# The opening of a chunked recurrence with three layers behind it, issued in another order

## The chip, the core and the metric

The kernel runs on one core of a Trainium2 chip. Its time is device time in microseconds (us), from the first instruction of the program to the last, and the number quoted for a kernel is the median of several executions. The engines are named as in the profile: PE is TensorE (matmuls, with PEld its weight loads), DVE is VectorE, ACT is ScalarE, POOL is GpSimd and SP is SyncE, which here only issues transfers. Each engine takes its instructions strictly in the order in which the program holds them.

## What is computed

A recurrence over 768 steps for 4 batches of 8 heads, with states of 40x40, whose output is the input of a gated two-matrix layer, whose output in turn goes through a layer of eight experts with top-1 routing. Cut to what matters:

```python
for t in range(S):                                   # 768 steps, per batch and head
    y[:, :, t] = einsum('bhd,bhde->bhe', rt, state)
    Sa = einsum('bhde,bhe->bhd', state, at)
    state = state * wt[:, :, None, :] - einsum('bhd,bhe->bhde', Sa, bt)
    state = state + einsum('bhd,bhe->bhde', vt, kt)
x = ((x @ w_a) * (x @ w_b)) @ w_out                  # 3072 tokens, 320 -> 1536 -> 320
out[mask] = gate_w * (relu(x[mask] @ w1[e]) @ w2[e]) # the expert of each token, 8 experts
```

## The kernel before

The recurrence is cut into 12 chunks of 64 steps. Within a chunk it becomes matmuls, and what one step does to the next inside the chunk is undone by inverting a triangular 64x64 matrix for each of the 32 pairs of batch and head. Work on chunk c runs in 24 slots; inside the same slots the program also prepares chunk c+2, inverts for a later chunk, and, from chunk 1 on, runs the first layer's matmuls (groups `pm`) for the chunk before. The order of PE, DVE, ACT and POOL is the order in which the Python code emits instructions. SP's transfers are put in order by a scheduler.

The steps that the text speaks of, for one chunk:

- `load_w`, `load_bk`: the decay `w` and the pair `b`,`k` are loaded (366 KB and 720 KB). `scans`: DVE runs a scan over `w` backwards, copies sums, takes reciprocals and scans again; before that POOL writes ones into the tile `d`, of which there is one.
- `scale_a`: the `a` of a chunk (two halves of 180 KB, each for a pair of batches) is scaled by POOL and spread by three transfers into the block tile `ablk`. There is one `ablk` for each pair, so the spread of the next chunk waits for the score matmuls of this one. `scale_bk`: DVE scales `b` and `k`.
- `scores`: 3 matmuls for each of 4 batches (`s1p`); ACT copies each result into `s`; POOL masks half of it; SP sends a quarter to DRAM as `nd` (four transfers of 64 KB for a chunk).
- `tinv`: `nd` is read back as `m`, twice 256 KB, each row to two partitions, and then DVE does the inverse as 31 pairs of a multiply and a subtract (`tmp`, `xt`), each on what the one before left. The last one sends `xt` to DRAM as `td` and reads it back into `s`.
- `t21a`, `t21b`: from the two inverted corners the third is made, with PE (`ta`, `tb`), ACT and DVE. Only then can the stages (`stage0` to `stage5`: `px`, `pu`, `pv`, `pp`, `p`, `py`, `pz`) of the chunk run.
- `rows` turns `bk` around (`kbp`, `kb`), `relayout` moves the decay into the layout of the output (`gp`, six transfers), `spans` lets ACT check the range of the decay (`junk`).

Beside this the two weight matrices of the first layer must be split into two 32-bit parts. `weight_steps` does that in 30 pieces; a piece is one load (`raw`, issued by ACT), four DVE instructions (`c_f`, `c_s`, `c_f`, `c_s`), three or more of ACT and two or three of POOL, and is emitted in four steps, which `conv.take(n)` deals out. The groups `pm` of chunk 0 run in chunk 1's slots and need the pieces in order.

Ahead of the slots, in `phase1`, stands the opening. In the kernel before it loads, scans and scales both chunks 0 and 1 first, then emits 20 steps of conversion, then chunk 0's scores, 5 steps, chunk 0's `rows`, 10 steps, chunk 1's scores, and then both inverses, which are dealt out on DVE in turns, together with 40 more steps. Thus 75 of the 120 steps stand ahead of chunk 0's slots, and 44 within them.

Of the kernel before, what the change touches and what calls it, by code (L numbers as in the profile page):

```python
# [8 lines left out]
F32 = mybir.dt.float32  # L9
# [123 lines left out]
def phase1(tc, I, cst, drm, psA, psM, ident, hT, mk_ident, wo, xs, span, tiny, down):  # L133
# [17 lines left out]
    sp = A.p2.tile([128, 2 * 256], I32, tag="raw", name="sp0"), A.p2.tile([128, 2 * 256], I32, tag="raw", name="sp1")  # L151
    A.load(0)
    A.load(1, M.room())
# [5 lines left out]
    A.setup()  # L159
    run(A.spans(1))  # L160
    A.scale_a(0, 0)
    A.scale_a(0, 1)
    run(A.scale_bk(0))
    run(A.scans(1))
    for pr in range(2):
        A.scale_a(1, pr, spread=False)
    run(A.scale_bk(1))
    n0, n1, n2, n3 = FIRST["conv0"]
    A.zero([A.vnt])
# [3 lines left out]
    run(conv.take(n0))  # L173
    for b in range(B):
        A.scores(0, b)
        if b % 2:
            A.spread_a(1, b // 2)
    run(conv.take(n1))
    for b in range(B):
        A.rows(0, b)  # L180
    tinv = A.tinv(0)
    run(conv.take(n2))
# [5 lines left out]
    mix(tinv[:n3], conv.take(FIRST["conv1"][0]) + [lambda b=b: A.rows(1, b) for b in range(B)])  # L188
    t1 = A.tinv(1, (uh, view(xt)))
    A.relayout(0)  # L190
    A.relayout(1)
    lead = FIRST["lead"]
    both = tinv[n3:n3 + lead]
    tinv = tinv[n3 + lead:]
    while tinv or t1:
        both += tinv[:1] + t1[:1]
        tinv, t1 = tinv[1:], t1[1:]
    mix(both, [lambda b=b: A.stage0(0, b) for b in range(2)] + conv.take(FIRST["conv1"][1]))
    run(A.spans(0, [t[:120, 0:L // 2].bitcast(F32) for t in sp]))
    units, tinv = [], []  # L200
    for c in range(NCH + 1):
# [9 lines left out]
        for i in range(24):  # L211
# [96 lines left out]
    if not down:  # L308
# [32 lines left out]
        0, 3, 3, 2, 3, 2, 2, 2, 2, 1, 2, 2,  # L341
        2, 2, 2, 4, 1, 1, 3, 0, 3, 0, 1, 1],
    "conv0": [20, 5, 10, 16], "conv1": [10, 30], "lead": 5, "early": 12, "load": 0, "bk": 5, "sa": [3, 5], "score": [9, 12, 13, 15], "row": [12, 13, 23, 23],
    "t21a": [8, 9, 14, 15], "t21b": [9, 12, 18, 16], "tinv": [0] * 24, "relayout": 17, "load_w": 18,
# [43 lines left out]
class Attention:  # L388
# [48 lines left out]
    def load(self, c, room=None):  # L437

        w, bk = room if room else (None, None)
        self.load_w(c, w)  # L440
        self.load_bk(c, bk)
# [58 lines left out]
    def scale_a(self, c, pr, spread=True):  # L500
        nc = self.nc
        st = self.st[c]
        t = self.p2.tile([120, 6 * 64], F32, tag=f"at{pr}", name=f"at{c}_{pr}", bufs=2 + pr)[:, :6 * C]
        sr = self.src("a", "a", c)[:, 6 * C * pr:6 * C * pr + 6 * C]
        nc.sync.dma_start(t, sr)
# [4 lines left out]
        if spread:  # L510
            self.spread_a(c, pr)

    def spread_a(self, c, pr):
        for m in range(3):
            self.nc.sync.dma_start(
                self.ablk[pr][m * D:(m + 1) * D, :, :, m, 0:C], self.st[c]["at"][pr][m * D:(m + 1) * D])
# [1208 lines left out]
```

## Time and profile before

| what | value |
|---|---|
| times shown, 3 runs | 1346.05, 1346.48, 1353.48 us; median 1346.48 |
| the profiled execution | 1349.91 us, of which the span of its instructions is 1348.2 |
| PE busy | 1192.2 us, 88% of the span |
| DVE busy | 679.9 us, 50% |
| ACT busy | 531.7 us, 39% |
| POOL busy | 444.0 us, 33% |
| granted TensorE clock, mean | 0.911 of full speed |

Over the whole span PE is the busy engine. The opening is another picture: in the first 100 us PE has next to nothing to do, and the other engines and the transfers decide when it can start. A row of a timeline gives start, duration, engine, line, operation, the tiles written and read, how many instructions are merged into the row, and in square brackets how long the engine had been idle and what ended that.

### The profile page before, as it was taken

Reading aid. Unit: us, or ns where it says so; the run is one execution under the profiler, and the core shown is the slowest. Engines: PE = TensorE matmul, PEld = TensorE weight load, DVE = VectorE, ACT = ScalarE, POOL = GpSimd, SP = SyncE. Lnnn points to the kernel's source line nnn. Section 1 sums busy time; section 2 is a strip of 40 time slices with the busy share of each in tenths; the row PEclk is TensorE's granted clock in tenths of the full one; section 3 lists DMA queues with packets and bytes.
Section 4 is the critical chain, followed back from the end, with each engine's and each line's share of the span. In section 5 each row is a group of like instructions: output and inputs, shape, how many; then the busy total and the mean of one; then the engine's idle time right before and its main releaser. Section 6 shows DMA issues by size and latency. Waiting matters only on the chain.

```text
span 1348.2 us, 27424 instructions
## 1 busy us (share of the span) xinstructions
PE 1192.2 (88%) x10474; PEld 1120.2 (83%) x10474; DVE 679.9 (50%) x1867; ACT 531.7 (39%) x1301; POOL 444.0 (33%) x488
## 2 busy tenths in 40 slices
PE   2306879997999998998999999999999989999995
PEld 2305779896888898898989999999999989999995
DVE  7487456563746465564746545312355685222321
ACT  3435544343343434352534333332333434444541
POOL 5443531232232323232421211112012255666650
PEclk9655559999998898998989999999799999999998
DMA  7363343537564748564544432217255635545420
GB/s 188 87 163 80 82 108 94 124 98 153 119 151 117 157 121 151 128 159 104 122 117 99 115 86 76 66 49 207 75 161 174 214 131 183 164 131 174 130 69 16
DMA packets 252908, 166.63 MB, mean 124 GB/s; under 512 B 158674, under 2 KB 236195, under 8 KB 252769
## 3 DMA queue, kind: packets, MB, share of 16 engines
q1 hardware_dynamic: 238545, 141.17, 41.1%
q0 software_dynamic: 9808, 15.76, 4.2%
q10 hardware_dynamic: 4416, 7.87, 2.1%
q8 instruction: 85, 1.39, 0.4%
q14 instruction: 54, 0.44, 0.1%
HBM read 111.76 MB, written 44.60 MB: 116 GB/s over the span
## 4 chain that ended last, share of the span: by engine, by line
PE 66%; DMA 15%; DVE 7%; issue 4%; POOL 3%; ACT 3%; SPq 1%; POOLq 0%; DVEq 0%; ACTq 0%
PE pm L964 19%; PE py L1101 8%; PE dn L1410 5%; PE u L1390 5%; DMA hT<-uh 4%; PE py L797 3%; PE px L716 3%; PE s1p L535 3%; PE p L775 3%; DMA at<-in_a 3%; PE pp L757 2%; PE py L793 2%; PE pu L735 2%; PE px L713 2%; PE ta L652 2%
## 5 line engine op out<-in xcount | busy, mean ns | idle before, releaser
L976 DVE TENSOR_TENSOR uh<-pm,ua 128x256 f32<-128x256 f32 x144 | 60.7, 422 | 249.3 <-PE pm L964 235.0
L964 PE MATMUL pm<-xl,wh 128*128 128x256 f32 x576 | 144.5, 333 | 0.5 <-POOL xl L943 0.5
L612 DVE TENSOR_TENSOR tmp<-m,xt 128x126 f32<-128x126 f32 (+22 forms) x372 | 116.4, 316 | 29.2 <-DMA m<-nd 14.6
L782 POOL TENSOR_SCALAR_AFFINE_SELECT s<-s 64x512 f32<-64x512 f32 x96 | 73.0, 760 | 140.7 <-ACT s L780 135.6
L964 PE MATMUL pm<-xh,wl 128*128 128x256 f32 x576 | 118.8, 289 | 0.0
L964 PE MATMUL pm<-xh,wh 128*128 128x256 f32 x576 | 118.0, 287 | 0.0
L618 DVE TENSOR_TENSOR xt<-xt,tmp 128x126 f32<-128x126 f32 (+22 forms) x372 | 111.0, 302 | 7.6
L1393 DVE SCALAR_TENSOR_TENSOR hl<-u,hh 128x384 fp32r<-128x384 f32 (+5 forms) x72 | 41.6, 581 | 140.7 <-ACT hh L1392 140.7
L943 POOL TENSOR_TENSOR xl<-xf,xh 128x192 fp32r<-128x192 f32 x48 | 28.7, 599 | 245.3 <-ACT xh L942 221.5
L967 ACT COPY ua<-pm 128x256 f32<-128x256 f32 x144 | 53.6, 372 | 124.1 <-PE pm L964 119.1
L652 PE MATMUL ta<-t,s 32*32 32x32 f32 x768 | 34.6, 202 | 69.0 <-DVE t L649 60.0
L964 PEld LDWEIGHTS pm<-xl,wh 128*128 128x128 f32 x576 | 90.3, 197 | 6.3 <-POOL xl L943 0.7
L1101 PE MATMUL py<-wh,hl 128*128 128x328 f32 x288 | 91.4, 317 | 2.1 <-DVE hl L1091 2.1
L1101 PE MATMUL py<-wl,hh 128*128 128x328 f32 x288 | 92.5, 321 | 0.6 <-DVE wl L1072 0.6
L964 PEld LDWEIGHTS pm<-xh,wh 128*128 128x128 f32 x576 | 92.4, 197 | 0.0
L964 PEld LDWEIGHTS pm<-xh,wl 128*128 128x128 f32 x576 | 92.3, 196 | 0.0
L1101 PE MATMUL py<-wh,hh 128*128 128x328 f32 x288 | 91.1, 316 | 0.0
L652 PEld LDWEIGHTS ta<-t,s 32*32 32x32 f32 x768 | 30.7, 117 | 71.5 <-ACT junk L472 41.4
L964 PE MATMUL pm<-xh,w 128*128 128x256 f32 x288 | 83.1, 289 | 0.0
L964 PE MATMUL pm<-xl,w 128*128 128x256 f32 x288 | 83.0, 288 | 0.0
L535 PE MATMUL s1p<-ablk,bk 120*128 120x192 f32 (+1 forms) x264 | 54.2, 350 | 26.0 <-DMA ablk<-at 21.6
L1410 PE MATMUL dn<-l,hh 128*128 128x320 f32 (+3 forms) x240 | 74.9, 312 | 0.0
(240 smaller groups left out, 3108.5 us busy)
## 6 DMA issues: line engine op xcount, KB each, us to landing
hT<-uh SPq DMA_DIRECT2D x72, 256.0 KB
hf<-hT SPq DMA_DIRECT2D x36, 512.0 KB
r<-in_moe_w SPq DMA_DIRECT2D x8, 1280.0 KB
r<-in_moe_w SPq DMA_DIRECT2D x8, 1024.0 KB
bk<-in_bk SPq DMA_DIRECT2D x11, 720.0 KB
xs<-zt SPq DMA_DIRECT2D x8, 805.0 KB
m<-nd SPq DMA_DIRECT2D x22, 256.0 KB
at<-in_a SPq DMA_DIRECT2D x24, 180.0 KB
```

The costliest lines, as they stand in the source:

```text
L535: nc.tensor.matmul(ps[:2 * C, 3 * g * C:(3 * g + n) * C], st["bk5"](b, g), self.ablk[b // 2][:, b % 2, g, 0:n, 0:C], start=True, stop=True)
L612: nc.vector.tensor_tensor(box[0], m[2 * s // R][:, s % (R // 2):s % (R // 2) + 1, s + 1:].to_broadcast([128, rows, n]), xt[:, :rows, s:s + ...
L618: nc.vector.tensor_tensor(xt[:, :rows, s + 1:], xt[:, :rows, s + 1:], box[0], op=ALU.subtract)
L652: nc.tensor.matmul(pa[R:C, R * h:R * h + R], s1[0:R, h, R:C], t11[:, h, :], start=True, stop=True)
L782: nc.gpsimd.affine_select(out=s2t[q * C:q * C + C], in_=s2t[q * C:q * C + C], pattern=[[0, 8], [1, C]], base=0, channel_multiplier=-1, com ...
L964: nc.tensor.matmul(p, l, r, start=(i == 0), stop=(i == len(seq) - 1))
L967: nc.scalar.copy(a, p)
L976: nc.vector.tensor_tensor(h[:, f % 2], p, a, op=ALU.mult)
L1101: self.nc.tensor.matmul(py, self.pair[i][l][:, k, s], self.W[r][:, first + k, cols], start=(first + k == 0 and n == 0), stop=(first + k == ...
L1390: nc.tensor.matmul(p, l, r, start=(i == 0), stop=(i == len(seq) - 1))
L1393: nc.vector.scalar_tensor_tensor(out=hl, in0=p, scalar=0.0, in1=hh.bitcast(F32), op0=ALU.max, op1=ALU.subtract)
L1410: nc.tensor.matmul(p, l[:, q], r[:, f], start=(f == 0 and i == 0), stop=(f == len(hs) - 1 and i == 2))
```

## The change

The opening is emitted in another order. First come chunk 0's `w`, its `a`, its `bk`, and then chunk 1's; `a` is now loaded by a function of its own. Chunk 0 is scanned, scaled, and its `a` is spread, one half by SP and the other by ACT's queue. Then chunk 0's scores and the request for its inverse follow at once, and only then chunk 1's scan and scaling, chunk 0's `rows`, 15 steps of conversion, chunk 1's scores, the first stage of two batches, the whole inverse of chunk 0 in one piece, and chunk 1's `rows`. Chunk 1's inverse is no longer part of the opening: it is dealt out over the slots 0 to 10 of chunk 0, and the `t21` steps of chunk 1 move to the slots 14 to 19. 72 steps of conversion now stand in chunk 0's slots, and the other 33 fall into the first eight of chunk 1. The check of chunk 0's decay moves from the end of the opening to slot 23 of chunk 0.

```diff
-    A.load(0)
-    A.load(1, M.room())
+    A.load_w(0)
+    for pr in range(2):
+        A.load_a(0, pr)
+    A.load_bk(0)
+    room = M.room()
+    A.load_w(1, room[0])
+    for pr in range(2):
+        A.load_a(1, pr)
+    A.load_bk(1, room[1])
...
     A.setup()
+    A.zero([A.vnt])
+    A.scale_a(0, 0)
+    A.scale_a(0, 1, queue=nc.scalar)
+    run(A.scale_bk(0))
     run(A.spans(1))
-    A.scale_a(0, 0)
-    A.scale_a(0, 1)
-    run(A.scale_bk(0))
+    for b in range(B):
+        A.scores(0, b)
+    tinv = A.tinv(0)
     run(A.scans(1))
     for pr in range(2):
-        A.scale_a(1, pr, spread=False)
+        A.scale_a(1, pr)
     run(A.scale_bk(1))
-    n0, n1, n2, n3 = FIRST["conv0"]
-    A.zero([A.vnt])
     A.begin(0)
     for pr in range(2):
         A.vload(0, pr)
-    run(conv.take(n0))
-    for b in range(B):
-        A.scores(0, b)
-        if b % 2:
-            A.spread_a(1, b // 2)
-    run(conv.take(n1))
     for b in range(B):
         A.rows(0, b)
-    tinv = A.tinv(0)
-    run(conv.take(n2))
+    run(conv.take(FIRST["conv0"]))
...
     for b in range(B):
         A.scores(1, b)
-    mix(tinv[:n3], conv.take(FIRST["conv1"][0]) + [lambda b=b: A.rows(1, b) for b in range(B)])
     t1 = A.tinv(1, (uh, view(xt)))
-    A.relayout(0)
-    A.relayout(1)
-    lead = FIRST["lead"]
-    both = tinv[n3:n3 + lead]
-    tinv = tinv[n3 + lead:]
-    while tinv or t1:
-        both += tinv[:1] + t1[:1]
-        tinv, t1 = tinv[1:], t1[1:]
-    mix(both, [lambda b=b: A.stage0(0, b) for b in range(2)] + conv.take(FIRST["conv1"][1]))
-    run(A.spans(0, [t[:120, 0:L // 2].bitcast(F32) for t in sp]))
-    units, tinv = [], []
+    for b in range(2):
+        A.stage0(0, b)
+    run(tinv)
+    for b in range(B):
+        A.rows(1, b)
+    for c in range(2):
+        A.relayout(c)
+    tinv = t1
+    units = []
...
+            if c == 0 and i == FIRST["span0"]:
+                sp = [A.p2.tile([128, 2 * 256], F32, tag="raw", name=f"sp{h}")[:120, 0:L // 2] for h in range(2)]
+                run(A.spans(0, sp))
...
-    "t21a": [8, 9, 14, 15], "t21b": [9, 12, 18, 16], "tinv": [0] * 24, "relayout": 17, "load_w": 18,
+    "t21a": [14, 14, 17, 17], "t21b": [16, 16, 19, 19], "tinv": [5, 6, 6, 6, 6, 6, 6, 6, 6, 6, 3] + [0] * 13, "relayout": 17, "load_w": 18,
...
+    def load_a(self, c, pr):
+        t = self.p2.tile([120, 6 * 64], F32, tag=f"at{pr}", name=f"at{c}_{pr}", bufs=2 + pr)[:, :6 * C]
+        self.nc.sync.dma_start(t, self.src("a", "a", c)[:, 6 * C * pr:6 * C * pr + 6 * C])
+        self.st[c]["raw_a", pr] = t
+
+    def scale_a(self, c, pr, queue=None):
...
-            self.nc.sync.dma_start(
+            (queue or nc.sync).dma_start(
                 self.ablk[pr][m * D:(m + 1) * D, :, :, m, 0:C], self.st[c]["at"][pr][m * D:(m + 1) * D])
```

Three places of the printed order show what moves. The first is ACT in the opening, where chunk 0's score copies stand (`s_0_0`, `s_0_1` are its two pairs of batches; `raw`, `c_s`, `wh` and `w` belong to the conversion). Before:

```order
L870 DMA raw_0_1_247<-in_moe_w_a 128x512
L363 ACTIVATE c_s<-raw_0_2_218 128x256
L370 ACTIVATE c_s,tiny<-c_s,tiny 128x256
L372 CAST w_0_249<-c_f 64x256
L372 CAST w_0_250<-c_f 64x256 x2
L382 CAST w_0_249<-c_f 64x256
L382 CAST w_0_250<-c_f 64x256
L543 COPY s_0_0_271<-s1p_0_267 128x512
L543 COPY s_0_0_271<-s1p_1_274 128x512
```

Now:

```order
L514 DMA ablk_95<-at_1_114 40x6x64 x3
L470 ACTIVATE junk,span<-w_r,wlim 120x384 x4
L542 COPY s_0_0_172<-s1p_0_168 128x512
L542 COPY s_0_0_172<-s1p_1_175 128x512
L542 COPY s_0_1_187<-s1p_2_183 128x512
L542 COPY s_0_1_187<-s1p_3_190 128x512
L568 COPY kb_0_229<-kbp_0_225 128x360
```

Five pieces of conversion stood ahead of the copies; now no piece does, and the spread of chunk 0's second half does instead.

The second place is SP's queue around chunk 0's `m`. Before (`at_0_173` and `at_1_176` are chunk 1's `a`, `s_0` is chunk 0):

```order
L515 DMA ablk_94<-at_0_173 40x6x64 x3
L550 DMA nd_116<-s_0_0_271 32x16x32 x2
L550 DMA nd_116<-s_0_1_289 32x16x32 x2
L515 DMA ablk_95<-at_1_176 40x6x64 x3
L603 DMA m_346<-nd_116 64x1x1024 x2
L550 DMA nd_123<-s_1_0_389 32x16x32 x2
```

Now (`at_0_123`, `at_1_125` are chunk 1's `a`):

```order
L581 DMA gp_492<-w_110 64x4x64 x2
L549 DMA nd_118<-s_0_0_172 32x16x32 x2
L549 DMA nd_118<-s_0_1_187 32x16x32 x2
L514 DMA ablk_94<-at_0_123 40x6x64
L602 DMA m_198<-nd_118 64x1x1024 x2
L514 DMA ablk_94<-at_0_123 40x6x64 x2
L514 DMA ablk_95<-at_1_125 40x6x64 x3
L581 DMA gp_499<-w_r 120x4x64
```

Chunk 0's `m` now has one spread transfer of chunk 1 ahead of it, and five behind it; chunk 0's six `gp` transfers have moved ahead of `nd`.

The third place is SP's queue around the sending of chunk 0's inverse (`td_0`). Before:

```order
L505 DMA at_1_1083<-in_a 120x384
L699 DMA r_0_1529<-in_r 120x192
L699 DMA r_1_1562<-in_r 120x192
L505 DMA at_1_1684<-in_a 120x384
L629 DMA td_0_103<-xt_347 512x1x32 x2
```

Now (`nd_129` and `m_0`, `m_1` are chunk 1's):

```order
L549 DMA nd_129<-s_1_1_329 32x16x32 x2
L581 DMA gp_499<-w_r 64x4x64
L597 DMA m_0_307<-nd_129 64x1x512
L597 DMA m_1_308<-nd_129 64x1x512
L597 DMA m_0_307<-nd_129 64x1x512
L597 DMA m_1_308<-nd_129 64x1x512
L628 DMA td_0_103<-xt_199 512x1x32 x2
```

Chunk 1's four `m` transfers stood far ahead of `td_0`, with the loads of chunks 2 and 3 between; now they stand directly ahead of it.

## Rows read from the trace of the kernel before

**Rows 1.** Timeline of the opening: SP's issues (start, duration, engine, line, tiles).

```profile
15.41 11.64 SPq L515 DMA_DIRECT2D ablk<-at  x6
38.75 1.95 SPq L550 DMA_DIRECT2D nd<-s  x4
43.94 1.29 SPq L603 DMA_DIRECT2D m<-nd  x2
62.46 2.40 SPq L598 DMA_DIRECT2D m<-nd  x4
64.91 10.52 SPq L582 DMA_DIRECT2D gp<-w  x5
104.41 2.63 SPq L629 DMA_DIRECT2D td<-xt  x4
```

**Rows 2.** Timeline of the opening: what the other engines do, and what they waited for.

```profile
8.78 1.78 DVE L496 TENSOR_TENSOR_SCAN w<-w,d 120x780 f32<-120x780 f32 x1
13.29 1.81 POOL L507 TENSOR_TENSOR at<-at,w 120x384 f32<-120x384 f32 x2 [4.85 <-DMA at<-in_a]
15.20 1.79 DVE L492 TENSOR_TENSOR_SCAN suf<-w_r,d 120x781 f32<-120x781 f32 x1 [2.21 <-POOL d L483]
19.36 2.36 POOL L507 TENSOR_TENSOR at<-at,w_r 120x384 f32<-120x384 f32 x2 [4.19 <-DVE w_r L496]
21.64 3.75 PE L535 MATMUL s1p<-ablk,bk 120*128 120x192 f32 x12 [21.64 <-DMA ablk<-at]
37.65 2.06 ACT L543 COPY s<-s1p 128x512 f32<-128x512 f32 x4
38.36 2.50 POOL L544 TENSOR_SCALAR_AFFINE_SELECT s<-s 64x512 f32<-64x512 f32 x4 [1.60 <-ACT s L543]
61.48 0.19 DVE L612 TENSOR_TENSOR tmp<-m,xt 128x31 f32<-128x31 f32 x1 [12.74 <-DMA m<-nd]
112.83 1.88 PE L652 MATMUL ta<-t,s 32*32 32x32 f32 x32 [41.32 <-DVE t L649]
```

**Rows 3.** The chain that ended last: two transfers on it (start, duration).

```profile
51.89 10.55 DMA nd<-s
63.66 12.10 DMA m<-nd
```

**Rows 4.** Busy time by stretch (from:to, length, PE, PEld, DVE, ACT, POOL, clock, DMA share, GB/s).

```profile
56.00:58.00 2.00, 0.00 (x0) 0.00 (x0) 0.00 (x0) 0.00 (x0) 0.00 (x0) 0.52 0.13 49
61.40:104.40 43.00, 1.89 (x16) 1.78 (x16) 36.70 (x136) 16.35 (x46) 19.90 (x19) 0.50 0.55 140
112.60:152.00 39.40, 35.49 (x370) 33.37 (x371) 24.98 (x46) 22.90 (x68) 15.60 (x20) 0.59 0.30 71
152.00:187.80 35.80, 26.39 (x182) 23.18 (x180) 13.29 (x31) 17.53 (x53) 14.09 (x21) 0.50 0.48 113
187.80:209.00 21.20, 21.20 (x138) 19.68 (x138) 15.70 (x37) 8.62 (x23) 7.90 (x10) 0.64 0.30 73
209.00:219.30 10.30, 10.30 (x98) 9.40 (x98) 7.44 (x23) 3.56 (x10) 2.26 (x4) 1.00 0.45 107
80.00:90.00 10.00, 0.00 (x0) 0.00 (x0) 10.00 (x46) 3.69 (x10) 5.11 (x3) 0.50 0.73 196
```

**Rows 5.** The inverse's multiplies, whole span: durations in ns, least/median/most.

```profile
L612 DVE TENSOR_TENSOR tmp<-m,xt x372: 134/270/944, 61.5 to 850.4; 128x126 f32<-128x126 f32 x18, 128x120 f32<-128x120 f32 x12, 128x110 f32<-128x110 f32 x12, 128x96 f32<-128x96 f32 x12
```

**Rows 6.** Conversion on DVE between 112.6 and 187.8 us (count, busy us, mean ns, idle before).

```profile
L365 DVE SCALAR_TENSOR_TENSOR c_f<-raw,c_f 128x256 int32<-128x256 int32 x11 | 7.6, 693 | 0.3
L376 DVE SCALAR_TENSOR_TENSOR c_s<-raw,c_s 128x256 f32<-128x256 uint32 x11 | 5.5, 504 | 0.3
L362 DVE TENSOR_SCALAR c_f<-raw 128x256 int32<-128x256 int32 x11 | 5.4, 487 | 5.5 <-DMA raw<-in_moe_w_b 5.5
L374 DVE TENSOR_SCALAR c_s<-c_f 128x256 int32<-128x256 int32 x10 | 3.2, 320 | 22.2 <-ACT c_s L370 22.0
```

**Rows 7.** Waits between 110 and 190 us (total us, times, longest).

```profile
ACT junk L472 <- DMA w<-in_w: 5.6, 1, 5.6
```

**Rows 8.** Conversion's first two DVE instructions, start to 70 us (least/median/most ns).

```profile
L362 DVE TENSOR_SCALAR c_f<-raw x12: 279/816/821, 22.5 to 69.9; 128x256 int32<-128x256 int32 x12
L365 DVE SCALAR_TENSOR_TENSOR c_f<-raw,c_f x11: 412/899/903, 23.1 to 65.6; 128x256 int32<-128x256 int32 x11
```

More of the change, by code (lines that the diff above doesn't have):

```diff
@@ L149, in phase1 @@
     nz = NE * XCAP * XW // 128 // 8
-    sp = A.p2.tile([128, 2 * 256], I32, tag="raw", name="sp0"), A.p2.tile([128, 2 * 256], I32, tag="raw", name="sp1")
-    A.load(0)
-    A.load(1, M.room())
+    A.load_w(0)
[7 more added lines that the diff above has]
+    A.load_bk(1, room[1])
     nc.scalar.activation(out=A.wlim, in_=A.wlim, func=AF.Copy)
@@ L340 @@
     "conv": [
-        0, 3, 3, 2, 3, 2, 2, 2, 2, 1, 2, 2,
-        2, 2, 2, 4, 1, 1, 3, 0, 3, 0, 1, 1],
-    "conv0": [20, 5, 10, 16], "conv1": [10, 30], "lead": 5, "early": 12, "load": 0, "bk": 5, "sa": [3, 5], "score": [9, 12, 13, 15], "row": [12, 13, 23, 23],
-    "t21a": [8, 9, 14, 15], "t21b": [9, 12, 18, 16], "tinv": [0] * 24, "relayout": 17, "load_w": 18,
[3 rows of a table added]
+    "t21a": [14, 14, 17, 17], "t21b": [16, 16, 19, 19], "tinv": [5, 6, 6, 6, 6, 6, 6, 6, 6, 6, 3] + [0] * 13, "relayout": 17, "load_w": 18,
     "span": 19, "scan": [21, 21, 22, 22, 23],
@@ L434, in src @@
         return self.I[name][c]
[L437 to L441, printed above, removed]
     def load_w(self, c, room=None):
@@ L498, in scans @@
         ]
-    def scale_a(self, c, pr, spread=True):
+    def load_a(self, c, pr):
[3 more added lines that the diff above has]
+    def scale_a(self, c, pr, queue=None):
         nc = self.nc
         st = self.st[c]
-        t = self.p2.tile([120, 6 * 64], F32, tag=f"at{pr}", name=f"at{c}_{pr}", bufs=2 + pr)[:, :6 * C]
-        sr = self.src("a", "a", c)[:, 6 * C * pr:6 * C * pr + 6 * C]
-        nc.sync.dma_start(t, sr)
+        if ("raw_a", pr) not in st:
+            self.load_a(c, pr)
+        t = st["raw_a", pr]
         tv = t.rearrange("p (s t) -> p s t", t=C)
@@ L509, in scale_a @@
         st["at"][pr] = t4
-        if spread:
-            self.spread_a(c, pr)
-    def spread_a(self, c, pr):
         for m in range(3):
-            self.nc.sync.dma_start(
+            (queue or nc.sync).dma_start(
                 self.ablk[pr][m * D:(m + 1) * D, :, :, m, 0:C], self.st[c]["at"][pr][m * D:(m + 1) * D])
```

3 rows, old and new, of the table FIRST are left out of this document.

## The prediction

> **What bounds the kernel now.** I read the busy shares by stretch first, then the timeline of the first 210 us, then the chain that ended last, then the groups of DVE's instructions. Over the whole span PE is the busy engine, but until 112.83 us it waits: that is when the first matmul of chunk 0's slots (`ta`) runs, after 41.32 us of idle time that ended with a DVE instruction [rows 2]. From there to 209 us, which I read as the end of the eighth slot of chunk 1, PE is busy 35.49 + 26.39 + 21.20 = 83.1 of 96.2 us, at about half clock, and DVE 24.98 + 13.29 + 15.70 = 54.0 [rows 4]. From 209 us on PE has no gap and the granted clock is 1.00 [rows 4]. The change touches nothing after that point. So two times are to be compared: when `ta` starts, and how long the stretch behind it takes once it holds the work that the opening no longer does.
>
> **How the opening reaches `ta` today.** Chunk 0's scores are there early (first matmul at 21.64 us), but ACT copies them only at 37.65 us, behind five pieces of conversion. `nd` goes out at 38.75, `m` is issued at 43.94, and DVE gets it at 61.48 [rows 1, 2]. While `m` moves, the transfers do 49 GB/s with 0.13 of the 16 engines busy [rows 4], that is two engines: I take it that `m` runs on two of them alone. What is issued behind it on the same queue then waits for these two. Chunk 1's `nd`, 64 KB pieces like those that were away within 5 us at 38.75, took 10.55 us on the chain; chunk 1's own `m`, issued from 62.46, landed at 75.76 [rows 1, 3].
>
> **The change, part by part: the new `ta`.**
> - Loads. `a` now comes ahead of most of the rest. POOL began to scale it at 13.29 after waiting 4.85 us for it; now the end of the scan at 8.78 + 1.78 = 10.56 decides, and two scalings of 0.9 end at 12.4. From the first spread issue to the scores took 21.64 - 15.41 = 6.2 us [rows 1, 2]: scores at 18.6.
> - Scores and copies. Half of the scores takes 3.75 us, all of them 7.5; the four copies take 2.06 and follow one by one [rows 2]. The last copy ends near 26.6, `nd` (1.95 us of issue) is out at about 28.
> - `m`. One spread transfer of chunk 1 now stands ahead of it on SP. That needs chunk 1's scaled `a`; the scan before it waits for POOL to write `d`, as it did at 15.20, and POOL is behind the four masks (2.50 us in all). Masks end near 27.3; from scan to scaling is 19.36 - 15.20 = 4.2; one scaling is 1.2 [rows 2]; with the issue `m` goes at 33.5 where it went at 43.94. Landing as before, 61.48 - 43.94 = 17.5 later: 51.
> - The inverse of chunk 0. 62 instructions at 0.27, the median [rows 5], are 16.7 us: it ends at 67.7. The 15 steps of conversion ahead of it lie in the wait for `m` and cost nothing; without that cover they would cost some 9 us.
> - What is late next. Five spread transfers of chunk 1 are queued behind `m`, so its scores start at 51 too and end at 58.5; with copies and `nd` its `m` is issued at 63 and lands 13.3 later, at 76. `td` of chunk 0 is ready at 67.7, but stands behind these four on the queue. DVE, in order, waits meanwhile at chunk 0's transposes. From the end of `td`'s issue to `ta` was 112.83 - 107.04 = 5.8 us [rows 1, 2]: `ta` at 82.
>
> So `ta` comes 31 us earlier. If `td` is not held it is 67.7 + 8.4 = 76; if chunk 0's `gp` transfers, now ahead of `nd`, block SP as five did for 10.52 us [rows 1], it is 93 or a little more. I take 82.
>
> **The stretch behind it.** Moved into it: chunk 1's inverse, 16.7 us of DVE, and 60 steps of conversion (75 stood ahead of `ta`, 15 now), that is 15 pieces. The price of a piece on DVE: the four means add up to 1.97 us [rows 6], while instructions overlap a little at their ends. From below: in the 43.00 us from 61.4, DVE was busy 36.70 with 136 instructions [rows 4]; with about 100 of the inverses at 0.27, 9.7 us stay for nine pieces, 1.1 each. From above: 0.82 and 0.90 for the first two, as mostly in the opening [rows 8], make 2.5. I take 1.75, near the mean of this very stretch. DVE then has 54.0 + 16.7 + 26.3 = 97 us to do, PE the same 83 as before.
>
> How densely? With inverse and conversion mixed, DVE was busy 36.70 of 43.00 us, 85% [rows 4]; but then PE did nearly nothing. With PE in it, it was busy 54.0 of 96.2, 56%. The work added is of the first kind, and the second share came of too little work, so I take 85%: 114 us. One wait is new: the check of chunk 0's decay in slot 23 needs a load that SP issues behind others, and ACT's copies for chunk 1 stand behind it. The nearest row is ACT's wait for a load of `w`, 5.6 us [rows 7]; bounds are nothing and twice that. The new end of the eighth slot: 82 + 114 + 6 = 202, against 209.
>
> Clock: TensorE was granted about half, the 1.2 GHz level, until shortly before 209, while PE worked without a gap from 187.8 [rows 4]. If PE has gaps there now, the 2.4 GHz level comes later. At most the 10.30 us behind 209 would double; I put 3.
>
> **Sum.** -31 for `ta`, then 114 + 6 against 96.2, which is +24, and +3 for the clock: -4. Against the profiled execution's 1349.91 that is 1346; the median of the runs shown is 3.4 us lower, so 1342.
>
> **Rivals.** A measurement of this kernel tells about 1%, 13.5 us, from no change.
> - *DVE stays nearly full.* Between 80 and 90 us it was busy 10.00 of 10.00 [rows 4]. At 92% and without the wait for the check the stretch takes 105: end at 187, no loss of clock, 1325. For it: there is always conversion to do. Against it: DVE's third instruction of a piece waited 22.0 us for ACT in ten pieces [rows 6].
> - *The moved work does not fit between.* That wait of 22.0 us is ACT standing behind PE's results. If each piece meets it, the 96.2 us stay and the moved work comes on top: 96.2 + 16.7 + 26.3 = 139, end at 221, with the clock +15: 1362, slower. It decides from a stretch of 127 us on (no gain), and by over 1% from 137. Against it: the inverse waits for no other engine.
> - *The pieces cost what they cost in the opening.* The first two instructions took 0.28 and 0.41 us at least, 0.82 and 0.90 mostly [rows 8], while POOL worked on the same pieces. At 2.5 us for all 26 pieces of the stretch DVE has 97 + 26 x 0.75 = 116.5, or 137 us at 85%: end at 225, +19: 1365, slower. The Trainium skill (SBUF — State Buffer, Who interferes with whom) states that VectorE with two inputs in SBUF, or in a two-port mode, and a GpSimd instruction that reads SBUF exclude each other for a whole instruction. By that rule fuller engines would meet more often; the trace agrees with 0.90 against 0.41. The mean of 1.97 in slots that hold both [rows 6] speaks against the full price.
> - *The opening gains little.* SP holds `nd` or `m` back and `ta` comes at 93 or 95: 13 us of the gain go, 1355.
>
> **How the numbers follow.** I give my forecast 0.37, the full DVE 0.29, work that does not fit 0.17, dear pieces 0.10, the late opening 0.07. The first and the last lie within 1%: 0.44. Faster by over 1% is 0.29, slower 0.27. The likeliest case alone spans 1334 to 1352 (DVE at 92 to 79% with the wait). The range for 8 in 10 reaches from a little below the full DVE to the dear pieces: 1320 to 1366.
>
> **What would show it.** In the new profile: ACT's copies of chunk 0's scores near 20 to 27 us; `m` landing near 51; the inverse running alone until 68; `td` issued then but its read-back only at about 78, with DVE idle for some 14 us; `ta` at 82; DVE at 85% or so until about 165; ACT waiting for the check's load at the turn to chunk 1; 1.00 as granted clock not before 200. Wrong would be: DVE busy under 73% behind `ta` (slower), `ta` before 76 or after 95, or a stretch after chunk 1's eighth slot that differs from before.

## The result and the profile after

The changed kernel takes 1368.06 us (median; 1366.18 to 1370.27) where the kernel before takes 1349.98 in the same runs: a ratio of 1.013, 95% interval 1.010 to 1.016. It is slower by 18 us; the forecast was 1342 and the range ended at 1366. The profiled execution took 1369.22 us with a span of 1367.5.

The opening first. In the timeline a row gives start, duration, engine, line, operation, tiles, count, and in brackets the idle time before it and what ended that:

```profile
14.28 3.17 ACTq L514 DMA_DIRECT2D ablk<-at  x3
20.14 5.56 PE L534 MATMUL s1p<-ablk,bk 120*128 120x192 f32 x24 [20.14 <-DMA ablk<-at]
25.73 0.59 ACT L542 COPY s<-s1p 128x512 f32<-128x512 f32 x1 [0.29 <-PE s1p L534]
27.26 1.78 DVE L490 TENSOR_TENSOR_SCAN suf<-w_r,d 120x781 f32<-120x781 f32 x1 [6.24 <-POOL d L481]
33.57 1.16 SPq L602 DMA_DIRECT2D m<-nd  x2
52.23 0.19 DVE L611 TENSOR_TENSOR tmp<-m,xt 128x31 f32<-128x31 f32 x1 [5.57 <-DMA m<-nd]
71.99 2.61 SPq L628 DMA_DIRECT2D td<-xt  x4
79.28 0.76 DVE L648 STREAM_TRANSPOSE t<-s 32x256 f32<-32x256 f32 x2 [7.33 <-DMA s<-td]
79.86 1.88 PE L651 MATMUL ta<-t,s 32*32 32x32 f32 x32 [17.43 <-DVE t L648]
```

Against [rows 1, 2], `m` is issued 10.4 us earlier and `ta` starts at 79.86 instead of 112.83: 33 us gained. All of it is lost again, and more. For that I use a mark that both traces have: the start of `px` for the second pair of batches of chunk 1, at 219.2 us before and 235.2 now. The forecast's mark, the end of that chunk's eighth slot, lies a few slots ahead of it. Busy time by stretch (from:to, length, PE, PEld, DVE, ACT, POOL with their instructions, granted clock, DMA share, GB/s), first two rows of the kernel before, which are new here:

```profile
0.00:112.80 112.80, 21.76 (x104) 20.55 (x104) 80.32 (x219) 44.21 (x119) 54.56 (x72) 0.66 0.57 142
112.80:219.20 106.40, 93.29 (x781) 85.55 (x781) 61.10 (x134) 52.40 (x151) 39.65 (x54) 0.61 0.37 89
```

and the same two stretches of the changed kernel:

```profile
0.00:79.90 79.90, 16.48 (x105) 15.95 (x106) 43.81 (x97) 18.47 (x44) 24.86 (x39) 0.73 0.46 115
79.90:235.20 155.30, 101.02 (x782) 91.80 (x782) 108.99 (x254) 77.21 (x225) 69.92 (x86) 0.58 0.45 110
```

Read DVE's column as busy and idle. Up to `ta` DVE was busy 80.3 and idle 32.5 us before; now it is busy 43.8 and idle 36.1. So `ta` did not come early because DVE waits less. It came early because 36.5 us of DVE's work were taken out ahead of it. Behind `ta` DVE was busy 61.1 and idle 45.3 us; now 109.0 and 46.3. The moved work has been laid on top of the old stretch, not into its gaps. The sum closes: -32.9 for `ta`, 155.3 - 106.4 = +48.9 for the stretch, and +3.3 behind the mark (1367.5 - 235.2 against 1348.2 - 219.2) make the 19.3 us between the two spans. The 3.3 us lie within the spread of the runs. PE's columns split the same 48.9 us another way: behind `ta` PE was without work for 13.1 us before and 54.3 now, 41.2 more, and its busy time grew by 7.7.

What DVE waited for between 79.9 and 235.2 us (total us, times, longest), and one wait of PE there:

```profile
DVE c_s L376 <- ACT c_s L372: 24.5, 14, 7.5
DVE w L489 <- ACT junk L470: 8.6, 2, 5.9
DVE c_f L364 <- DMA raw<-in_moe_w_a: 4.4, 1, 4.4
DVE c_f L364 <- DMA raw<-in_moe_w_b: 4.2, 5, 2.0
PE pu L734 <- ACT xs L719: 10.5, 1, 10.5
```

Of DVE's 46.3 us of idle time, 33.1 are waits for a step of the conversion (first, third and fourth row). 8.6 are waits for ACT's check of a later chunk's decay. In the last row PE waits for ACT, which stood behind the load of chunk 0's check. None is a wait of the inverse. The prices of the moved instructions (count, busy us, mean ns, idle before), 79.9 to 225 us for the conversion's four and 79.9 to 198 us for chunk 1's inverse:

```profile
L367 DVE SCALAR_TENSOR_TENSOR c_f<-raw,c_f 128x256 int32<-128x256 int32 x26 | 16.5, 635 | 0.5
L378 DVE SCALAR_TENSOR_TENSOR c_s<-raw,c_s 128x256 f32<-128x256 uint32 x27 | 13.7, 508 | 0.5
L364 DVE TENSOR_SCALAR c_f<-raw 128x256 int32<-128x256 int32 x26 | 12.4, 477 | 9.5 <-DMA raw<-in_moe_w_a 4.4 <-DMA raw<-in_moe_w_b 4.2 <-POOL wl L386 0.6
L376 DVE TENSOR_SCALAR c_s<-c_f 128x256 int32<-128x256 int32 x26 | 8.2, 315 | 25.2 <-ACT c_s L372 24.5
L617 DVE TENSOR_TENSOR xt<-xt,tmp 128x126 f32<-128x126 f32 (+22 forms) x31 | 12.3, 395 | 0.5
L611 DVE TENSOR_TENSOR tmp<-m,xt 128x126 f32<-128x126 f32 (+22 forms) x31 | 11.1, 357 | 0.3
```

A piece costs DVE 0.635 + 0.508 + 0.477 + 0.315 = 1.94 us. (These are durations; DVE's instructions overlap a little, so its busy time is less than their sum.)

### The profile page after: what moved, and what is told of

Its sections match the earlier page's. It is cut to its first block, busy times and chain, and to the rows that moved or that the text cites. A ratio compares the mean times of both kernels' runs of the same rounds, so it can differ in the third digit from the quotient of the medians.

```text
span 1367.5 us, 27430 instructions
## 1 busy us (share of the span) xinstructions
PE 1196.0 (87%) x10474; PEld 1123.5 (82%) x10474; DVE 693.5 (51%) x1867; ACT 531.1 (39%) x1301; POOL 444.3 (32%) x488
## 4 chain that ended last, share of the span: by engine, by line
PE 63%; DMA 17%; DVE 7%; issue 4%; POOL 3%; ACT 3%; SPq 1%; ACTq 0%; POOLq 0%; DVEq 0%
PE pm L963 18%; PE py L1100 8%; PE dn L1409 5%; PE u L1389 5%; DMA hT<-uh 4%; PE py L796 3%; PE px L715 3%; PE pp L756 2%; PE p L774 2%; PE s1p L534 2%; DMA at<-in_a 2%; PE pu L734 2%; PE py L792 2%; PE px L712 2%; PE ta L651 2%
## 5 line engine op out<-in xcount | busy, mean ns | idle before, releaser
L611 DVE TENSOR_TENSOR tmp<-m,xt 128x126 f32<-128x126 f32 (+22 forms) x372 | 120.9, 325 | 21.2 <-DMA m<-nd 5.6
L617 DVE TENSOR_TENSOR xt<-xt,tmp 128x126 f32<-128x126 f32 (+22 forms) x372 | 114.3, 307 | 8.5
L781 POOL TENSOR_SCALAR_AFFINE_SELECT s<-s 64x512 f32<-64x512 f32 x96 | 71.6, 746 | 141.2 <-ACT s L779 135.5
L1100 PE MATMUL py<-wh,hl 128*128 128x328 f32 x288 | 91.9, 319 | 1.8 <-DVE hl L1090 1.8
L543 POOL TENSOR_SCALAR_AFFINE_SELECT s<-s 64x512 f32<-64x512 f32 x48 | 34.0, 708 | 127.7 <-ACT s L542 124.5
```

The lines of the kernel that those rows point to most:

```text
L611: nc.vector.tensor_tensor(box[0], m[2 * s // R][:, s % (R // 2):s % (R // 2) + 1, s + 1:].to_broadcast([128, rows, n]), xt[:, :rows, s:s + ...
L617: nc.vector.tensor_tensor(xt[:, :rows, s + 1:], xt[:, :rows, s + 1:], box[0], op=ALU.subtract)
L781: nc.gpsimd.affine_select(out=s2t[q * C:q * C + C], in_=s2t[q * C:q * C + C], pattern=[[0, 8], [1, C]], base=0, channel_multiplier=-1, com ...
L1100: self.nc.tensor.matmul(py, self.pair[i][l][:, k, s], self.W[r][:, first + k, cols], start=(first + k == 0 and n == 0), stop=(first + k == ...
```

## The experiments

Each kernel is compared with the kernel before on the same chip. The table holds the account that the text below speaks of: when `ta` starts, when the mark is reached, how long the stretch between them is, and how long DVE was idle ahead of `ta` and behind it (length of the stretch less DVE's busy time).

| kernel | median us | ratio to before (95%) | `ta` | mark | stretch | idle ahead | idle behind |
|---|---|---|---|---|---|---|---|
| before (1347.5 to 1350.0 in the four sets) | 1349.98 | 1 | 112.8 | 219.2 | 106.4 | 32.5 | 45.3 |
| changed | 1368.06 | 1.013 (1.010-1.016) | 79.9 | 235.2 | 155.3 | 36.1 | 46.3 |
| e1 check early | 1358.91 | 1.0075 (1.0047-1.0103) | 81.1 | 230.5 | 149.4 | 37.3 | 39.6 |
| e2 three raw buffers | 1357.87 | 1.0082 (1.0053-1.0111) | 80.1 | 231.7 | 151.6 | 36.4 | 39.5 |
| e3 inverse 1 ahead | 1373.82 | 1.0192 (1.0128-1.0255) | 91.9 | 248.8 | 156.9 | 32.4 | 62.3 |
| e4 early scores only | 1354.86 | 1.0054 (1.0027-1.0081) | 122.5 | 226.3 | 103.8 | 40.6 | 43.6 |
| e5 = e1 + e2 | 1354.25 | 1.0056 (1.0034-1.0078) | 80.0 | 224.3 | 144.2 | 36.2 | 31.5 |
| e6 = e5, gaps filled | 1349.33 | 1.0021 (1.0003-1.0040) | 88.9 | 220.7 | 131.8 | 34.4 | 30.8 |
| e7 changed, `m` spread | 1315.01 | 0.9752 (0.9719-0.9786) | 69.4 | 219.9 | 150.4 | 24.7 | 39.3 |
| e8 before, `m` spread | 1292.91 | 0.9593 (0.9556-0.9630) | 101.8 | 201.5 | 99.7 | 21.0 | 37.8 |
| e9 third step free | 1362.32 | 1.0108 (1.0072-1.0145) | 81.5 | 234.1 | 152.6 | 37.6 | 42.8 |
| e10 inverse 1 in slots only | 1356.68 | 1.0061 (1.0039-1.0082) | 120.1 | 228.9 | 108.8 | 50.3 | 33.2 |
| e11 = e5 + e9 | 1349.90 | 1.0012 (0.9985-1.0038) | 79.6 | 217.8 | 138.1 | 36.0 | 29.8 |
| e12 = e8 + third step free | 1283.82 | 0.9519 (0.9481-0.9557) | 97.9 | 192.6 | 94.7 | 17.3 | 31.9 |

### What the moved parts cost in the slots

**The check (e1).** It goes back to the end of the opening; everything else is the changed kernel.

```diff
     A.load_bk(1, room[1])
+    sp = [A.p2.tile([128, 2 * 256], F32, tag="raw", name=f"sp{h}")[:120, 0:L // 2] for h in range(2)]
+    check0 = A.spans(0, sp)
...
         A.relayout(c)
+    run(check0)
...
-            if c == 0 and i == FIRST["span0"]:
-                sp = [A.p2.tile([128, 2 * 256], F32, tag="raw", name=f"sp{h}")[:120, 0:L // 2] for h in range(2)]
-                run(A.spans(0, sp))
```

> The check of chunk 0's decay alone goes back to the end of the opening, with its load issued behind chunk 1's loads. In the changed kernel ACT waited 6.0 us for that load at the turn to chunk 1, spent 4 x 0.8 us on it, and PE stood 10.5 us for ACT's xs. Theory C (the check is a loss of its own): PE's wait for xs goes, the mark at which px of chunk 1's second half starts (235.2 us) comes 8 to 11 us earlier, and the time falls from 1368 to 1357-1360. Theory H (hand-over: the conversion's steps, dealt between ACT, DVE and POOL in order, set the pace there anyway): the wait moves on to another engine, and the time falls by less than 4 us, to 1364 or more.

The time is what the first theory gave, and PE's wait for `xs` behind 160 us shrinks from 10.5 us to

```profile
PE pu L734 <- ACT xs L719: 3.1, 1, 3.1
```

The mark comes only 4.7 us earlier, not 8 to 11. So the check is a loss of its own, about half a per cent, but it is not most of the 48.9 us.

**The loads of `raw` (e2).** From slot 12 on a third buffer, two pieces ahead.

```diff
-            pool, tag = (self.p2, ("xh", "xl")[j % 2]) if self.early else (self.pc, "raw")
+            pool, tag, kw = (self.p2, ("xh", "xl")[j % 2], {}) if self.early else (self.pc, "raw", {})
+            if not self.early and j % 3 == 0:
+                pool, tag, kw = self.p2, "wo", dict(bufs=1)
...
-            for d in range(3 if self.early else 2):
+            for d in range(3):
```

> Only change against the changed kernel: from slot 12 of chunk 0 on the weights' raw tiles have three buffers and are loaded two pieces ahead, not one (the third buffer is the tile that chunk 1's inverse has left). Theory L (late loads): DVE and ACT waited some 8.6 and 7.0 us for raw between 80 and 225 us; these waits go, and with them some of the steps behind, so the time falls by 5 to 9 us to 1359-1363. Theory H (hand-over): the steps are limited by the chain ACT square, DVE multiply, ACT copy, POOL subtract of each piece and the time falls by less than 3 us.

A gain of about the expected size: DVE's idle time behind `ta` falls by 6.8 us. Both edits together are e5:

> The two edits of the last kernels together: chunk 0's check back at the end of the opening, and three raw buffers from slot 12 on. Alone they gave 9 and 10 us against the changed kernel's 1368. If they take away different idle time of DVE, the gains add up: 1347 to 1351, and DVE's idle time up to the start of px of chunk 1's second half falls from 82.4 us (changed kernel; 76.9 and 75.9 with one edit) to about 70. If both take away the same idle time near the turn to chunk 1, one of them is enough: 1355 to 1358, idle time 75 or more.

In the trace the two add up: 36.2 + 31.5 = 67.7 us of idle time up to the mark, where the first case had about 70. The median came out between the two cases, at 1354.25.

**The inverse (e3, e10).** e3 takes chunk 1's inverse out of the slots and runs it straight behind chunk 0's:

```diff
-    tinv = t1
+    run(t1)
+    tinv = []
...
-"tinv": [5, 6, 6, 6, 6, 6, 6, 6, 6, 6, 3] + [0] * 13
+"tinv": [0] * 24
```

> Only change against the changed kernel: chunk 1's whole inverse stands directly behind chunk 0's, ahead of the slots, and not dealt out over slots 0 to 10. It then takes what chunk 0's took, 17.6 us, and the first ta comes at 97 to 99 instead of 79.9. If DVE's amount of work decides (the forecast's sum), the slots give these 17 us back and no more: 1368, within 3 us. If the inverse is dearer in the slots, where its instructions took 0.41 us against 0.285 alone (25.2 us against 17.6), the time falls by about 8 us to 1360. If only the density of the conversion decides and the inverse lies in its gaps there, the time grows by 10 to 17 us, to 1378-1385.

`ta` moves by 12 us only, since 7.3 us of the gap behind `td` are filled, and the stretch behind it does not get shorter at all:

```profile
91.90:248.80 156.90, 99.69 (x781) 90.69 (x781) 94.64 (x192) 77.42 (x225) 68.33 (x86) 0.59 0.43 107
```

The stretch is 156.9 us with the inverse taken out, 155.3 with it in; DVE is merely idle 16 us longer there. The later `ta` reaches the mark in full (248.8 us, +13.6); the time shows 6 to 8 us of it, and the intervals of the two ratios overlap. None of the three cases is met in full. The third, that the inverse lies in gaps of the slots, is the nearest, and it is right about the stretch.

In e10 the inverse stays in the slots, and the conversion is dealt as before.

```diff
-    for b in range(2):
-        A.stage0(0, b)
-    run(tinv)
-    for b in range(B):
-        A.rows(1, b)
+    mix(tinv, [lambda b=b: A.rows(1, b) for b in range(B)] + [lambda b=b: A.stage0(0, b) for b in range(2)] + conv.take(FIRST["conv1"]))
...
-    "conv": [
-        0, 2, 2, 2, 2, 2, 2, 3, 3, 3, 3, 4,
-        4, 4, 4, 4, 4, 4, 4, 3, 4, 3, 3, 3],
-    "conv0": 15, "span0": 23,
+    "conv": [
+        0, 3, 3, 2, 3, 2, 2, 2, 2, 1, 2, 2,
+        2, 2, 2, 4, 1, 1, 3, 0, 3, 0, 1, 1],
+    "conv0": 15, "conv1": 60,
```

> One half of the move alone: chunk 1's inverse is dealt out over slots 0 to 10 as in the changed kernel, but the conversion is dealt as in the kernel before (75 steps ahead of the slots, 44 in them), and the check stands at the end of the opening. If the inverse lies free of charge in the slots (taking it out did not shorten them) and only the pieces cost there, ta comes at 108 to 112, the stretch behind it takes what it took before (106 us), px of chunk 1's second half starts at 214 to 218, and the time is 1343 to 1347, no slower than the kernel before. If the inverse costs its own 17.6 to 25 us in the slots, that mark comes at 233 or later and the time is 1360 or more.

Busy time ahead of `ta` and behind it:

```profile
0.00:120.10 120.10, 16.22 (x105) 15.81 (x106) 69.83 (x157) 46.68 (x124) 53.19 (x72) 0.66 0.52 131
120.10:228.86 108.76, 95.24 (x781) 87.45 (x781) 75.61 (x196) 50.51 (x145) 40.62 (x53) 0.59 0.36 85
```

The half of the expectation that this run was made for came true: with 62 more DVE instructions in it the stretch takes 108.8 us where it took 106.4, and DVE's busy time rises from 61.1 to 75.6 while its idle time falls from 45.3 to 33.2. **The inverse is almost free in the slots.** The other half failed: `ta` comes at 120.1, not at 108 to 112, and the time, 1356.68, lies between the two cases. Two rows of DVE's timeline say where, by the idle time in brackets:

```profile
63.98 0.29 DVE L371 TENSOR_SCALAR c_s<-c_f 128x256 int32<-128x256 int32 x1 [9.07 <-ACT c_s L367]
119.52 0.76 DVE L643 STREAM_TRANSPOSE t<-s 32x256 f32<-32x256 f32 x2 [4.56 <-DMA s<-td]
```

The first piece behind chunk 1's scores waits 9.07 us for ACT, which stands behind the copies of those scores (ACT itself waited 7.9 us for one of them); the inverse is queued behind that piece on DVE and waits with it.

**The hand-over within a piece (e9, e11, e12).** DVE's third instruction overwrites the tile in which ACT checks the squares. It gets a tile of its own; ACT's tile needs one buffer then.

```diff
-    sq = pool.tile([128, n], F32, tag="cs", name="c_s")
+    sq = pool.tile([128, n], F32, tag="cs", name="c_s", bufs=1 if small else 2)
+    ex = pool.tile([128, n], F32, tag="cx", name="c_x", bufs=2) if small else sq
...
-    nc.vector.tensor_scalar(sq.bitcast(I32), T, -0x800000, None, op0=ALU.bitwise_and)
+    nc.vector.tensor_scalar(ex.bitcast(I32), T, -0x800000, None, op0=ALU.bitwise_and)
```

> Only change against the changed kernel: DVE's third instruction of a conversion piece writes a tile of its own, no longer the one in which ACT has just checked the squares, so it need not wait for ACT (24.5 us in 14 waits behind ta). Theory H (this hand-over sets what a piece costs in the slots, 2.5 us against 1.94 us of DVE's own time): the wait goes, some 0.4 us a piece are saved over 26 pieces, and the time falls by 8 to 13 us to 1355-1360. Rival: the wait only moves on, to POOL's sum of the piece or to the next load of raw, and the time falls by less than 4 us.

The wait of 24.5 us is gone, and most of it turns up one step on. The group of the first instruction of a piece, behind `ta` (busy, mean ns, idle before it):

```profile
L365 DVE TENSOR_SCALAR c_f<-raw 128x256 int32<-128x256 int32 x26 | 12.7, 487 | 26.0 <-DMA raw<-in_moe_w_b 17.5 <-POOL wl L387 3.3 <-ACT w L385 2.3
```

It now waits 26.0 us where it waited 9.5. The time falls by 5.7 us by the medians and by 3 by the ratios, half a per cent at most, and the intervals of the ratios overlap; the stretch is 2.7 us shorter. That is nearer to the rival. With the check and the third buffer as well:

> The changed kernel with three edits: the check back at the end of the opening, three raw buffers, and the third instruction free of ACT. The first two together gave 1354. If the wait for ACT is idle time apart from theirs, 8 us or more come off again: 1342 to 1346, at or below the kernel before. If it is the same idle time, or DVE is full by then, 1351 or more.

Busy time in its stretch:

```profile
79.60:217.80 138.20, 97.93 (x782) 89.27 (x782) 108.43 (x253) 73.81 (x216) 70.67 (x86) 0.60 0.47 117
```

What DVE still waits for in this stretch:

```profile
DVE w L490 <- ACT junk L471: 14.1, 2, 7.7
DVE c_f L365 <- POOL wl L387: 8.7, 3, 3.2
```

1349.9 is again between the cases, and no longer to be told from the kernel before. The stretch is 138.1 us, 17.2 less than in the changed kernel, and 29.3 more than in e10, which has the inverse in the slots too but 15 pieces fewer (11 of the first instruction behind `ta`, not 26). That is 1.95 us a piece, about what a piece costs DVE itself, 1.94. Against e10 DVE is busy 32.8 us longer in the stretch and idle only 3.4 us less. e10 has waits of its own, and in e11 the wait for ACT's check of a later chunk's decay has grown to 14.1 us, so this is an account, not a measured price; it says that with the three waits gone the pieces still cost their whole length.

### What the opening gains by itself

**Early scores alone (e4).** The new order of loads, scans and scores, but both inverses and 75 steps ahead of the slots, 40 instructions of chunk 0's inverse first and the rest dealt in turns.

```diff
-    run(tinv)
+    mix(tinv[:n3], conv.take(FIRST["conv1"][0]) + [lambda b=b: A.rows(1, b) for b in range(B)])
...
+    both, tinv = [], tinv[n3:]
+    while tinv or t1:
+        both += tinv[:1] + t1[:1]
+        tinv, t1 = tinv[1:], t1[1:]
+    mix(both, [lambda b=b: A.stage0(0, b) for b in range(2)] + conv.take(FIRST["conv1"][1]))
...
+    "conv0": 15, "conv1": [20, 40], "lead": 40,
```

> The new order of loads, scan, spread and scores of chunk 0 alone: chunk 0's m lands at 52 us, but both inverses and 75 steps of conversion stay ahead of the slots and the check stays at the end of the opening, as in the kernel before. DVE then has 62 more instructions of inverse (17.6 us) and 60 steps (15 pieces at 1.9, 29 us) to do after 52 us than the changed kernel, beside chunk 0's inverse of 17.6: at 85% density ta comes at 52 + 64/0.85 = 127, later than before (112.8), and the time is 1350 + 14 = 1364, if DVE is the bound of the whole opening. If the work fills the idle time that DVE has ahead of 52 us and the density is as in the opening before, ta comes at 100 to 105 and the time is 1338 to 1342, below the kernel before.

`ta` comes at 122.5 us, 9.7 later than before, and DVE's idle time ahead of it is 40.6, not 32.5. It is the first case, with a smaller loss in the time. The earlier `m` brings nothing as long as DVE has the same work to do and gets to it no sooner: in [rows 8] the conversion starts at 22.5 us, in the changed kernel at 34.6, since chunk 1's scan waits for POOL behind the masks (6.24 us in the timeline of the opening).

**Gaps filled (e6).** On top of e5, five pieces move from chunk 1's slots to the two places where DVE waited for `m` and for `td`.

```diff
-    "conv0": 15,
+    "conv0": 23, "conv1": 12,
...
     run(tinv)
+    run(conv.take(FIRST["conv1"]))
```

> As the kernel before it in this list, and five pieces of conversion (20 steps) move from chunk 1's slots into the opening: two ahead of chunk 0's inverse, where DVE waited 5.6 us for m, and three behind it, where DVE waited 7.3 us for the inverse to come back from DRAM. Theory D (the time follows DVE's busy plus its idle time up to the middle of chunk 1): up to 10 us of idle time are filled, and the time falls by 6 to 10 us against the kernel without this edit. Theory W (the waits between ACT, DVE and POOL in the slots set the pace, whatever is taken out): it falls by less than 3 us.

The stretch gets shorter by 12.4 us, 2.5 for each piece, and `ta` comes 8.9 later, 1.8 for each. The net 3.6 at the mark, and 4.9 in the median, is real but under the 6 to 10 expected: the idle time ahead of `ta` fell by 1.8 us only. So five pieces cost 2.5 us each in the slots and 1.8 in the opening.

### The transfer that the opening waits for

**`m` spread (e7, e8).** The prediction took it that `m` runs on two DMA engines. Each of its transfers is cut into one for each copy, so that 32 rows are outermost and not 2. Chunk 1's transfers, in the other branch, are cut in the same way.

```diff
-                nc.sync.dma_start(
-                    t[64 * k:64 * k + 64],
-                    st["nd"][k].rearrange("s j t -> s (j t)")[None].to_broadcast([2, 32, R * R]))
+                for p in (64 * k, 64 * k + 32):
+                    nc.sync.dma_start(t[p:p + 32], st["nd"][k])
```

> Only change against the changed kernel: m is read back by one transfer of 32 rows for each copy (twice as many transfers), not by one whose outer size is 2. The prediction took it that m runs on two of the 16 DMA engines alone. If so, m lands at 38 to 43 us instead of 52, chunk 0's inverse starts at 47 behind its conversion, its td is not held behind chunk 1's m, ta comes at 72 to 75 instead of 79.9, and chunk 2's m no longer delays the raw loads (7.9 and 5.0 us on the chain behind 150 us): 1368 falls to 1354-1362. If latency and not the two engines made m's 17.5 us, ta stays within 2 us of 79.9 and the time within 4 us of 1368.

> The same edit of m's read-back in the kernel before, nothing else. There DVE waited 12.74 us for chunk 0's m, in one piece. If the two engines are what m's 17.5 us are made of, that wait falls to 0 to 3 us, ta comes at 101 to 105 instead of 112.8, and the time falls by 8 to 12 us to 1336-1340, more than any order of the opening gave. If it is latency, nothing moves: 1347.6, within 3 us.

The timeline of the kernel before with this edit (issue of `m`, and its first use):

```profile
43.91 3.84 SPq L602 DMA_DIRECT2D m<-nd  x4
51.81 0.19 DVE L609 TENSOR_TENSOR tmp<-m,xt 128x31 f32<-128x31 f32 x1 [3.05 <-DMA m<-nd]
```

Busy time while `m` moves in it:

```profile
46.00:50.00 4.00, 4.00 (x16) 4.00 (x16) 2.59 (x5) 2.92 (x8) 2.20 (x3) 0.50 0.94 196
```

`m` is there 7.9 us after its first issue, not 17.5, and the engines are 0.94 busy, not 0.13 [rows 4] (other transfers run in both). `ta` moved as expected in e8, to 101.8, and further than expected in e7, to 69.4. The times fell by far more than either theory had, by 4 and nearly 4 per cent, because the edit holds for all twelve chunks. From the mark to `px` of the last chunks, before and with the edit:

```profile
219.20:874.00 654.80, 624.59 (x6461) 577.77 (x6460) 360.19 (x1020) 253.67 (x690) 168.26 (x219) 0.96 0.51 119
```

```profile
201.50:820.20 618.70, 612.01 (x6462) 566.27 (x6461) 362.25 (x1020) 253.70 (x689) 164.45 (x219) 0.99 0.55 127
```

36.1 of the gain lie here. PE has 6.7 us without work there, not 30.2, and works 12.6 us less for the same instructions, at a higher granted clock (0.99 on the mean instead of 0.96). Two waits for loads issued on the same queue show what was held up, before and with the edit:

```profile
POOL at L507 <- DMA at<-in_a: 34.9, 4, 14.5
DVE bk L525 <- DMA bk<-in_bk: 27.4, 8, 5.4
```

```profile
POOL at L507 <- DMA at<-in_a: 8.9, 4, 2.6
DVE bk L525 <- DMA bk<-in_bk: 2.2, 1, 2.2
```

PE's waits for the inverses of these chunks, before and with the edit:

```profile
PE ta L652 <- DVE t L649: 15.9, 4, 9.3
PE ta L652 <- DVE tmp L612: 7.9, 4, 3.5
```

```profile
PE ta L649 <- DVE t L646: 2.4, 2, 1.8
```

From 23.8 us to 2.4, they are most of the 23.5 us by which PE's time without work fell. No wait of DVE for `m` itself stands in the list of the kernel before for this stretch. So what a slow `m` costs there is read as coming through the loads behind it; no run sends `m` alone on another queue.

With `m` spread the changed order is still the slower one, 0.975 against 0.959, and the account is the same: `ta` is 32 us earlier, the stretch behind it 51 us longer. e12 frees the third step in the better of the two:

> The kernel before with m's read-back spread over more engines (1293) and the third instruction of a piece free of ACT. The kernel before shows 29.3 us of such waits up to the middle of chunk 1, 22 of them in the slots. If they set the pace there, 5 to 10 us come off: 1283 to 1288. If PE or the loads take over, 1290 or more.

It came out at 1283.82, the fastest kernel here, 4.8% below the kernel before. The edit that brought half a per cent at most in the changed order (e9) brings 9 us here, 0.7%, with 11 pieces in the stretch instead of 26; here the stretch itself gets 5.0 us shorter and `ta` comes 3.9 us earlier.

## Why the prediction was wrong

**The new `ta`: right.** Scores at 20.1 (said: 18.6), the last copy at 25.7 to 26.3 (26.6), `m` issued at 33.6 (33.5) and there at 52.2 (51), the read-back behind `td` at 77.3 (78), `ta` at 79.9 (82). Too short was the inverse alone, 16.7 us; it took from 52.2 to 72.0 with 17.6 us of DVE time (31 instructions at 314 and 31 at 255 ns, and gaps between them). So DVE then idled 7.3 us, not 14. The late inverse cost nothing, since `td` was held behind chunk 1's `m`, as the forecast had it: from the first issue of that `m` to the first read-back behind `td` it is 14.3 us here and 14.2 in e11, where `td` went out 0.5 us later, and with `m` spread (e7) the read-back came 3.1 us after the issue of `td` and not 5.3.

**What was moved: nearly right.** By the forecast's own terms DVE's work behind `ta` up to the mark would be 61.1 + 16.7 + 26.3 = 104 us; it is 109.0. A piece costs 1.94 us, where 1.75 was taken (the four means of [rows 6] add up to 2.00, not to 1.97; 1.97 is the busy time over 11). The inverse in the slots costs 23.4 us, where 16.7 was taken and 17.6 are measured for chunk 0's alone. The same 62 instructions take 0.377 us on the mean in the slots and 0.284 alone, while POOL did 3.7 of 20 us. In e10, with 15 pieces fewer in the stretch, it is still 0.367. The timeline shows what makes the difference:

```profile
99.50 0.26 DVE L617 TENSOR_TENSOR xt<-xt,tmp 128x110 f32<-128x110 f32 x1
99.72 0.72 POOL L382 TENSOR_TENSOR c_f<-c_f,c_s 128x256 f32<-128x256 f32 x1 [0.61 <-DVE c_s L378]
99.80 0.79 DVE L611 TENSOR_TENSOR tmp<-m,xt 128x126 f32<-128x126 f32 x1
100.40 0.98 POOL L510 TENSOR_TENSOR at<-at,w 120x384 f32<-120x384 f32 x1
100.62 0.90 DVE L617 TENSOR_TENSOR xt<-xt,tmp 128x126 f32<-128x126 f32 x1
101.65 0.27 DVE L611 TENSOR_TENSOR tmp<-m,xt 128x120 f32<-128x120 f32 x1
```

The instruction of 0.79 us began while one of POOL ran and ended 0.15 us after it; the next one did the same, 0.14 us after POOL. All 16 of the 62 that took more than 0.55 us began beside a running instruction of POOL. This bears out the rule of the Trainium skill that the prediction named (SBUF — State Buffer, Who interferes with whom); no run here takes POOL's work away.

**How densely: wrong, and this step decided.** "The work added is of the first kind, and the second share came of too little work, so I take 85%: 114 us." DVE's share in the stretch is 109.0 / 155.3 = 70%, below the 73% that the prediction named as the sign of a slower kernel. The 85% came from a stretch in which inverse and conversion ran mixed and PE did nothing. In the slots only one of the two behaves like that. The inverse needs nobody: e10 and e3 show that it goes into DVE's idle time, 2.4 us and less than nothing. A piece does not: five pieces taken out shorten the stretch by 2.5 us each (e6), and with the three waits removed fifteen still seem to cost 1.95 each (e11). The 48.9 us are then 17.2 of waits (e11), 2.4 of the inverse (e10) and 29.3 of pieces; this last term is the difference that is left. That pieces cost their whole length is shown; why is argued: a piece needs a load, ACT, DVE and POOL in turn, each of them behind the slots' own work, and a wait that is removed turns up at the next step (e9).

**The rival that came true.** "The moved work does not fit between" described it: the old 96.2 us stay and the work comes on top. It held for the pieces and not for the inverse, so its argument was half right, and its 1362 was 6 us short. It had a chance of 0.17. The evidence that it rested on, the wait of 22.0 us for ACT [rows 6], grew only to 24.5 and was worth half a per cent at most when it was removed (e9). The "dear pieces" gave 1365, but their instructions did not get dear.

**The check and the loads.** 6 us were put down for the check. PE waited 10.5, and e1 gave 0.55% back, about 7 us: right in kind and size. That the loads of `raw` would come late was not in the sum; e2 gave back 0.5%.

**Clock.** 3 us were put down. In the stretch PE's busy time rose from 93.3 to 101.0 us for the same instructions, at a mean granted clock of 0.58 instead of 0.61. So 7.7 of the 48.9 us went by while PE worked more slowly; how much of that reached the end was not tried apart. The forecast's sign held: the clock was still 0.50 (the 1.2 GHz level) from 190 to 200 us, rose behind that, was down to 0.70 ahead of the mark, where PE had gaps, and was 0.98 to 1.00 (the 2.4 GHz level) only from 235 us on, where PE had none.

**The thought behind it.** The forecast took 31 us of an earlier `ta` as a gain and then asked what the moved work costs. The account of DVE's idle time asks at once whether anything was gained: ahead of `ta` it rose from 32.5 to 36.1 us. e4 shows the same from the other side.

## What to carry to other kernels

When work is moved from one stage to another on an engine that takes its instructions in order, compare idle time and not the time at which the next stage starts: a stage that starts earlier by as much as was taken out of it has gained nothing. Before work is put into the gaps of a busy stage, ask whose gaps they are: in this kernel a chain that stays on one engine fitted there, and one that is handed through four queues did not. And a transfer that is late in the opening is worth a look at how many engines it runs on, ahead of any order of instructions around it.

## What the hardware showed

The read-back with an outer size of 2 was known to be slow in the opening; that it cost 4% over the kernel, two thirds of it behind the mark, was not expected. The Trainium skill (DMA: Bandwidth & Descriptors, Rules for kernel authors) says that an outermost dimension smaller than 16, its example being a leading broadcast of copies, confines a transfer to at most that many engines, and advises a size that is a multiple of 16. The traces agree: 0.13 of 16 engines against 0.94, `m` there after 7.9 us and not 17.5, and the ratio of 0.959. That rule speaks of the transfer itself; the larger part here is what happens behind the mark, where the waits shown are those for loads issued behind it.
